# Loading an output projection as four consecutive rows per partition, in a kernel that streams a key and value cache

## The chip, the cores and the metric

The kernel runs on one core of one Trainium2 chip. The metric is the device time of one execution in microseconds (us). Before the change three runs gave a median of 1267.47 us (1267.24 to 1267.68). A profile records one execution: its "span" runs from the first to the last instruction and is some 2 us shorter than the time quoted for the same run (1266.8 against 1268.64 us before the change).

## The reference, cut to what matters

One token passes through attention over a cache of 65,536 positions, and beside it through a small gated network, which the change doesn't touch.

```python
Hq, Hkv, Sk, Dh = 16, 8, 65536, 256      # 16 query heads, 8 key/value heads
q = (x @ wq).reshape(B, Sq, Hq, Dh).transpose(0, 2, 1, 3)
scores = einsum("bhqd,bhkd->bhqk", q, repeat(k_cache, 2, axis=1)) * Dh ** -0.5
o = einsum("bhqk,bhkd->bhqd", softmax(scores), repeat(v_cache, 2, axis=1))
a = o.transpose(0, 2, 1, 3).reshape(B, Sq, Hq * Dh) @ wo      # wo is 4096 x 448, bf16
return g * a + (1 - g) * b
```

Keys and values are 537 MB in bf16 and each byte is read once. `wo` is 3.7 MB.

## The kernel before

The work goes through 8 pairs of query heads (`REP = 2` heads share one key/value head), four tiles each, 32 tiles in all. A tile is 8 MB of keys and 8 MB of values. SyncE issues all large loads, in this order:

```python
for j in range(NP):                       # 32 tiles
    if j >= 1:
        eng.wait_ge(sem_tr[NB - 1], BODY * (j - 1) + DC)   # half of the last tile's keys are read
    load(kring, A_k_cache, j, ...)        # 8 MB
    ...
    eng.wait_ge(sem_pv, j)                # the last tile's values are used up
    load(vbuf, A_v_cache, j, ...)         # 8 MB
    ...
    if j % PPH == 0:                      # first tile of a head pair
        g = j // PPH
        if g >= 1:
            eng.wait_ge(s_proj, g)        # the last head pair's projection is done
        eng.dma_start(wo_sb[:, :, :],
                      A_wo[g * REP * DH:(g + 1) * REP * DH, :].rearrange(
                          "(h p j) n -> p h (j n)", h=REP, j=2)).then_inc(sem_wo, 16)
```

So partition `p` of `wo_sb` gets rows 2p and 2p+1 of the first head of the pair and rows 2p and 2p+1 of the second. These are two stretches of 1792 B, read 229 KB apart and written side by side.

At the end of a head pair the sums over the positions lie in `accs`. Two fp32 products bring them into columns, one column per head and parity of d. VectorE divides them by the softmax sums, and 16 small products multiply them with `wo`:

```python
def by_d(dst):                                        # TensorE
    for dj in range(2):
        ins = pe.matmul(dst[:, dj * REP:(dj + 1) * REP], accs[:, dj:DH:2], sel[:, :], ...)
    return ins
def project():
    for hh in range(REP):
        for dj in range(2):
            j = dj * REP + hh
            for q in range(NCG):
                ins = pe.matmul(prj[32 * q:32 * q + 1, 0:WG], oTn[:, j:j + 1],
                                wo_sb[:, hh, dj * DM + q * WG:dj * DM + (q + 1) * WG], ...)
    ins.then_inc(s_proj, 1)

def finish_head(g):                                   # VectorE
    take(...)                                         # accs, densum, rden = 1 / densum
    vec.tensor_copy(qcur[:, :, :], qT[:, :, bass.ds(g * REP + REP, REP)])
    vec.drain()
    vec.wait_ge(s_sel, g + 1)
    by_head(acc[:, SELC:NACC])                        # oTn = sums * rden
```

Below, "head" means one such pair.

The softmax here doesn't subtract the row's maximum and nothing guards it: scores larger than these inputs give would overflow.

Of the kernel before, what the change touches and what calls it, by code (L numbers as in the profile page):

```python
# [8 lines left out]
ALU = mybir.AluOpType  # L9
# [3 lines left out]
def bass_gated_mix__gqa_block_cached__mixer_token_mlp__decode_kernel(  # L13
# [15 lines left out]
    f32 = mybir.dt.float32  # L29

    H = A_k_cache.shape[1]
    T = A_k_cache.shape[2]
    DH = A_k_cache.shape[3]
    DM = A_x.shape[-1]
    HQ = A_wq.shape[1] // DH
    REP = HQ // H
    F = B_w1.shape[1]
    FT = F // 128
    P = 128
# [28 lines left out]
    NCG = 4  # L68
    WG = DM // NCG
# [15 lines left out]
    SELC = DENC + 2 * NT  # L85
    NACC = SELC + 2 * REP
# [4 lines left out]
    with ctx:  # L91
        def sb(shape, dt, name):
            return ctx.enter_context(nc.sbuf_tensor(name, shape, dt))

        def psum(shape, dt, name):
            return ctx.enter_context(nc.psum_tensor(name, shape, dt))

        def new_sem(name):
            return ctx.enter_context(nc.semaphore(name))
# [11 lines left out]

        wo_sb = sb([P, REP, 2 * DM], bf16, "wo_sb")

        early = vbuf[:, :, :].rearrange("p n d -> p (n d)")
        early_f = vbuf_f[:, :, :].rearrange("p n d -> p (n d)")
        wq_a = early[:, 0:WF * NQ].rearrange("p (j n) -> p j n", j=WF)
# [23 lines left out]
        oTn = sb([P, 2 * REP], bf16, "oTn")  # L140
        accs = sb([P, SELC], f32, "accs")
        sel = sb([P, REP], f32, "sel")
        zrow = sb([1, NACC], bf16, "zrow")
        rden = sb([P, REP], f32, "rden")
        densum = sb([P, REP], f32, "densum")
        b2_b = sb([1, 1], bf16, "b2_b")
        stat = sb([1, 8], f32, "stat")
        statb = sb([1, 8], bf16, "statb")
# [16 lines left out]
        acc = psum([P, 512], f32, "acc")  # L165
        prj = psum([P, 512], f32, "prj")
# [8 lines left out]
        sem_wo = new_sem("sem_wo")  # L175
# [8 lines left out]
        s_sel = new_sem("s_sel")  # L184
# [14 lines left out]
        s_oTn = new_sem("s_oTn")  # L199
# [9 lines left out]
        def src(cache, j, n0=0, n1=NV):  # L209
            g, m = divmod(j, PPH)  # L210
            s = cache[0, g, m * BODY * CH:(m + 1) * BODY * CH, :].rearrange("(p n) d -> p n d", p=P)
            return s[:, n0:n1, :].rearrange("p n d -> p (n d)")

        @block.sync
        def _(eng):
            eng.dma_start(wq_a.rearrange("p j n -> p (j n)"),  # L216
                          A_wq[0:WF * P, :].rearrange("(p j) n -> p (j n)", p=P)).then_inc(sem_wq, 16)
            eng.dma_start(wq_b, A_wq[WF * P:DM, :].rearrange("r (a n) -> (r a) n", a=2)  # L218
                          ).then_inc(sem_wq, 16)
            def load(dst, cache, j, n0, n1, at, sem):  # L220
                eng.dma_start(dst[:, at + n0:at + n1, :].rearrange("p n d -> p (n d)"), src(cache, j, n0, n1)  # L221
                              ).then_inc(sem, 16)

            for j in range(NP):
                last = j == NP - 1
                if j >= 1:
                    eng.wait_ge(sem_tr[NB - 1], BODY * (j - 1) + DC)
                load(kring, A_k_cache, j, 0, HV if last else NV, HV * (j % 2), sem_k)
                if last:
                    load(kring, A_k_cache, j, HV, NV, HV, sem_kb)  # L230
                if j == 0:
                    eng.wait_ge(s_q, 1)
                    eng.wait_ge(s_hb, 1)
                else:
                    eng.wait_ge(sem_pv, j)
                load(vbuf, A_v_cache, j, 0, NLATE if last else NV, 0, sem_v)
                if last:
                    for (n0, n1), sem in zip(pieces, sem_vp):
                        load(vbuf, A_v_cache, j, n0, n1, 0, sem)
                if j % PPH == 0:  # L240
                    g = j // PPH
                    if g >= 1:
                        eng.wait_ge(s_proj, g)
                    eng.dma_start(wo_sb[:, :, :],
                                  A_wo[g * REP * DH:(g + 1) * REP * DH, :].rearrange(
                                      "(h p j) n -> p h (j n)", h=REP, j=2)).then_inc(sem_wo, 16)
            eng.wait_ge(s_fin, 1)
            eng.dma_start(out_ap, out_g[0:P:P // NCG, :]).then_inc(sem_out, 16)
            eng.wait_ge(sem_out, 16)
# [13 lines left out]
        def _(pe):  # L263
# [76 lines left out]
            def piece_wait(n):  # L340
                for (n0, _), sem in zip(pieces, sem_vp):
                    if n == n0:
                        pe.wait_ge(sem, 16)
# [11 lines left out]
            def by_d(dst):  # L355
                for dj in range(2):
                    ins = pe.matmul(dst[:, dj * REP:(dj + 1) * REP], accs[:, dj:DH:2], sel[:, :],
                                    start=False, stop=True, skip_group_check=True)
                return ins

            def clear(bank):
                pe.matmul(bank, ones_sq[0:1, :], zrow[0:1, 0:bank.shape[-1]], start=True, stop=True,
                          skip_group_check=True)

            def project():
                for hh in range(REP):
                    for dj in range(2):
                        j = dj * REP + hh
                        for q in range(NCG):
                            ins = pe.matmul(prj[32 * q:32 * q + 1, 0:WG], oTn[:, j:j + 1],  # L370
                                            wo_sb[:, hh, dj * DM + q * WG:dj * DM + (q + 1) * WG],
                                            start=False, stop=True, skip_group_check=True)
                ins.then_inc(s_proj, 1)


            def tail():
                late_values(*pieces[0])
                pe.wait_ge(s_cp, H)
                by_d(sps[:, 0, 0:2 * REP])
                late_values(pieces[1][0], NV).then_inc(s_late, 1)  # L380
                pe.wait_ge(sem_wo, 16 * H)
                pe.wait_ge(s_oTn, H)
                project()

            pe.sem_inc(sem_qk, 2)
            pe.wait_ge(sem_ident, 1)
# [11 lines left out]
            for dj in range(2):  # L398
                for h in range(HQ):
                    j = dj * HQ + h  # L400
                    col = h * DH
                    a, cb = divmod(col, HALF)
                    for kt in range(WF):
                        pe.matmul(sps[:, 1, j:j + 1], wq_a[:, kt, col + dj:col + DH:2],
                                  xcol[:, kt:kt + 1], start=(kt == 0), stop=False)
                    ins = pe.matmul(sps[:, 1, j:j + 1], wq_b[:, cb + dj:cb + DH:2],
                                    xcol[:, WF + a:WF + a + 1], start=False, stop=True)
# [13 lines left out]
            with nc.Fori(0, H, 1, engines=on, head_slot={pe.engine: 0}) as g:  # L421
                with nc.Fori(0, PPH, 1, engines=on, head_slot={pe.engine: 0}) as m:
                    j = pe.snap(g * PPH + m, min_val=0, max_val=NP - 1)
                    c0 = pe.snap(j * BODY, min_val=0, max_val=NC)
                    u16 = pe.snap(j * 16 + 16, min_val=16, max_val=16 * NP)
                    keys(c0, j, u16, pe.snap(x2_reg, min_val=0, max_val=NV))
                    values(j, c0, u16)
                    with pe.If(j < FT):
                        pe.wait_ge(s_pb, j + 1)
                        for q in range(NCG):  # L430
                            pe.matmul(prj[32 * q:32 * q + 1, WG:2 * WG], w2cur[:, :],  # L431
                                      gu[:, q * WG:(q + 1) * WG], start=False, stop=True, skip_group_check=True)
                    pe.reg_sub(x2_reg, NV, x2_reg)
                with pe.If(g < H - 1):
                    pe.wait_ge(s_cp, g + 1)
                    clear(acc[:, 0:NACC])
                    by_d(acc[:, SELC:NACC]).then_inc(s_sel, 1)
                    pe.wait_ge(sem_wo, pe.snap(g * 16 + 16, min_val=16, max_val=16 * H))
                    pe.wait_ge(s_oTn, g + 1)
                    project()  # L440

        @block.vector
        def _(vec):
# [101 lines left out]
            def by_head(src):  # L545
                po_v = src.rearrange("p (dj hh) -> p dj hh", dj=2, hh=REP)
                r_v = rden[:, :].rearrange("p (o hh) -> p o hh", o=1).broadcast_to((P, 2, REP))
                vec.tensor_tensor(oTn[:, :].rearrange("p (dj hh) -> p dj hh", hh=REP), po_v, r_v,  # L548
                                  op=ALU.mult).then_inc(s_oTn, 1)

            def finish_head(g):
                take(vec.snap(g * PPH + PPH, min_val=PPH, max_val=NP))
                vec.tensor_copy(qcur[:, :, :], qT[:, :, bass.ds(g * REP + REP, REP)])
                vec.drain()
                vec.wait_ge(s_sel, g + 1)
                by_head(acc[:, SELC:NACC])

            vec.wait_ge(s_q, 1)
            vec.tensor_copy(qT[:, :, :].rearrange("p a b -> p (a b)"), sps[:, 1, 0:2 * HQ])
# [8 lines left out]
            with nc.Fori(0, H - 1, 1, engines=on) as g:  # L568
                with nc.Fori(0, PPH, 1, engines=on) as m:
                    j = vec.snap(g * PPH + m, min_val=0, max_val=NP)  # L570
# [12 lines left out]
            with nc.Fori(NC - NCPH, NC, BODY, engines=on) as c0:  # L583
                for k in range(BODY):
# [6 lines left out]
                                     op0=ALU.mult, op1=ALU.add).then_inc(s_fin, 1)  # L591
# [69 lines left out]
```

## Time and profile before

| | |
|---|---|
| time, median of 3 | 1267.47 us |
| span of the profiled execution | 1266.8 us |
| duration of the packet records, summed, per DMA engine | 1261.7 us |
| TensorE busy | 911.8 us (72%) |
| one tile, from key landing to key landing | 38.70 us; 39.90 us where a wo load lies between |

The page of the kernel before, from its slice, queue and group parts. The DMA row gives tenths of busy time in 40 slices of the span. A group line gives, after the first bar, busy us and mean ns of one instruction, and after the second the idle time ahead of them and what ended most of it:

```profile
DMA  9999999999999999999999999999999999999998
DMA packets 12365, 544.39 MB, mean 430 GB/s; under 512 B 1344, under 2 KB 3394, under 8 KB 3778
q1 hardware_dynamic: 12264, 544.22, 99.5%
q8 instruction: 8, 0.13, 0.0%
L278 PE MATMUL kst<-ident,kring 128*128 128x128 f32 x4096 | 561.6, 298 | 310.5 <-DMA kring<-in_A_k_cache_dram 308.6
```

The DMA engines are busy throughout (9 tenths or more in every slice but the last; the packets of q1 took 99.5% of the span), and TensorE waits 308.6 us in total for key loads. The kernel is bound by its transfers.

The chain of waits of the kernel before, at three successive tiles. Columns: start in us, duration in us, what ran:

```profile
190.25 6.14 PE kst L278 x32
...
230.15 6.66 PE kst L278 x32
...
268.86 6.09 PE kst L278 x32
```

The keys of a tile are read as soon as they land (0.12 us later in this chain), so the differences are the time that the transfers of one tile take: 39.90 us with the wo load in between, then 38.71 us without. This step is the ruler of this study. It repeats within 0.02 us from head to head, while whole runs differ by 0.4 us and more.

The timeline of the kernel before, at the end of the first head (the number in brackets is idle time ahead of the instruction, and what ended it):

```profile
180.73 0.55 PEld L357 LDWEIGHTS acc<-sel,accs 128*128 128x128 f32 x4
181.78 0.37 PE L370 MATMUL prj<-wo_sb,oTn 128*1 128x112 bf16 x16 [0.41 <-DVE oTn L548]
182.19 0.38 SPq L244 DMA_DIRECT2D wo_sb<-in_A_wo_dram  x1
190.25 1.97 PE L278 MATMUL kst<-ident,kring 128*128 128x128 f32 x8 [8.10 <-DMA kring<-in_A_k_cache_dram]
```

After the projection TensorE has nothing to do for 8.1 us.

### The profile page before, as it was taken

How to read it: one execution, taken by the hardware profiler on the slowest of the kernel's cores; microseconds unless marked ns; L12 is line 12 of the kernel's file. 1: busy time of each engine (PE TensorE's matmuls, PEld its weight loads, DVE VectorE, ACT ScalarE, POOL GpSimd, SP SyncE). 2: the span in 40 equal slices, each digit the busy share in tenths (PEclk: the TensorE clock that was granted, in tenths of full speed). 3: DMA queues.
4: the chain of work that ended last, by engine and by line, in shares of the span. 5: the costliest groups of instructions: out<-in, count | busy, mean ns of one | idle time of the engine just before them, and what ended most of it. 6: DMA issues, size and time to landing. Idle time of an engine off the chain costs nothing.

```text
span 1266.8 us, 38663 instructions
## 1 busy us (share of the span) xinstructions
PE 911.8 (72%) x17041; PEld 862.0 (68%) x17041; DVE 418.1 (33%) x741; ACT 537.4 (42%) x786; POOL 0.9 (0%) x7
## 2 busy tenths in 40 slices
PE   1886678766787666787666876768767688666698
PEld 1776668766677666686666876658766578665687
DVE  2433334333344233443222332223322233331233
ACT  0543345533355333454334553335533345432455
POOL 0000000000000000000000000000000000000000
PEclk9988789788898788888788888789887788887989
DMA  9999999999999999999999999999999999999998
GB/s 411 430 417 430 432 430 441 430 432 432 430 441 430 432 430 432 441 430 432 430 432 441 430 432 430 432 441 430 430 432 430 443 430 430 432 430 443 430 416 350
DMA packets 12365, 544.39 MB, mean 430 GB/s; under 512 B 1344, under 2 KB 3394, under 8 KB 3778
## 3 DMA queue, kind: packets, MB, share of 16 engines
q1 hardware_dynamic: 12264, 544.22, 99.5%
q8 instruction: 8, 0.13, 0.0%
q10 hardware_dynamic: 90, 0.01, 0.0%
q14 instruction: 3, 0.02, 0.0%
HBM read 544.22 MB, written 0.00 MB: 430 GB/s over the span
## 4 chain that ended last, share of the span: by engine, by line
DMA 68%; PE 30%; issue 1%; SPq 0%; DVE 0%; ACT 0%; ACTq 0%
DMA kring<-in_A_k_cache_dram 66%; PE kst L278 25%; PE sps L298 5%; DMA vbuf<-in_A_v_cache_dram 2%; PE acc L330 1%; PE sps L350 0%; SPq L221 0%; PE acc L322 0%; PE prj L370 0%; ACT pT L615 0%; SPq L218 0%; SPq L216 0%; DVE out_g L590 0%; PE prj L431 0%; DVE oTn L548 0%
## 5 line engine op out<-in xcount | busy, mean ns | idle before, releaser
L278 PE MATMUL kst<-ident,kring 128*128 128x128 f32 x4096 | 561.6, 298 | 310.5 <-DMA kring<-in_A_k_cache_dram 308.6
L626 ACT ACTIVATE ktT<-kst 128x1024 bf16<-128x1024 bf16 x512 | 499.6, 1021 | 668.1 <-PE kst L278 667.8
L278 PEld LDWEIGHTS kst<-ident,kring 128*128 128x128 f32 x4096 | 511.8, 155 | 320.2 <-issue 318.0
L532 DVE COPY ktT<-kst 128x1024 bf16<-128x1024 bf16 x512 | 354.3, 692 | 771.4 <-PE kst L278 748.1
L298 PEld LDWEIGHTS sps<-qcur,ktT 128*128 128x128 bf16 x8192 | 237.8, 96 | 6.5 <-issue 3.9
L298 PE MATMUL sps<-qcur,ktT 128*128 128x2 bf16 x8192 | 236.7, 163 | 3.5 <-issue 3.5
L330 PE MATMUL acc<-vbuf,pT 128*2 128x256 bf16 x4064 | 144.2, 310 | 3.5 <-issue 2.8
L330 PEld LDWEIGHTS acc<-vbuf,pT 128*2 128x2 bf16 x4064 | 107.4, 95 | 31.9 <-issue 3.3
L615 ACT ACTIVATE pT<-sps 128x32 f32 x256 | 51.8, 202 | 18.6 <-PE sps L298 18.6
L322 PE MATMUL acc<-pT,ones_sq 128*128 128x32 bf16 x256 | 11.7, 178 | 12.3 <-ACT pT L615 12.3
L322 PEld LDWEIGHTS acc<-pT,ones_sq 128*128 128x128 bf16 x256 | 8.6, 97 | 15.2 <-ACT pT L615 14.9
L632 ACT ACTIVATE z_b<-z_b 128x448 bf16<-128x448 bf16 x14 | 8.1, 577 | 20.5 <-DVE z_b L519 20.5
L537 DVE COPY accs<-acc 128x288 f32<-128x288 f32 x8 | 3.7, 458 | 39.6 <-PE acc L330 39.6
L394 PE MATMUL acc<-vbuf 42*128 42x42 bf16 x1 | 0.2, 216 | 8.6 <-DMA b_b<-in_B_b_dram 8.6
L523 DVE TENSOR_SCALAR z_b<-z_b 128x448 bf16<-128x448 bf16 x14 | 3.9, 277 | 6.8 <-ACT z_b L632 6.8
L394 PEld LDWEIGHTS acc<-vbuf 42*128 42x128 bf16 x1 | 0.1, 100 | 8.7 <-DMA b_b<-in_B_b_dram 8.7
L525 DVE TENSOR_TENSOR gu<-wtmp,z_b 128x448 bf16<-128x448 bf16 x14 | 5.5, 393 | 1.0
L517 DVE TENSOR_TENSOR z_b<-u_b,wtmp 128x448 bf16<-128x448 bf16 x14 | 5.5, 393 | 1.0
L513 DVE TENSOR_TENSOR z_b<-wtmp,u_b 128x448 bf16<-128x448 bf16 x14 | 5.5, 393 | 1.0
L511 DVE TENSOR_TENSOR wtmp<-u_b 128x448 bf16<-128x448 bf16 x14 | 5.5, 392 | 1.1
L507 DVE TENSOR_SCALAR wtmp<-hbT,params 128x448 bf16<-128x448 bf16 x14 | 4.7, 337 | 2.6 <-issue 2.6
L509 DVE TENSOR_SCALAR u_b<-wtmp,params 128x448 bf16<-128x448 bf16 x14 | 4.7, 336 | 2.6 <-issue 2.6
(84 smaller groups left out, 76.5 us busy)
## 6 DMA issues: line engine op xcount, KB each, us to landing
kring<-in_A_k_cache_dram SPq DMA_DIRECT2D x2, 4096.0 KB, 22.7
vbuf<-in_A_v_cache_dram SPq DMA_DIRECT2D x1, 6144.0 KB, 24.3
wo_sb<-in_A_wo_dram SPq DMA_DIRECT2D x8, 448.0 KB, 28.6
vbuf<-in_A_wq_dram SPq DMA_DIRECT2D x1, 3072.0 KB, 10.3
vbuf<-in_A_v_cache_dram SPq DMA_DIRECT2D x1, 1024.0 KB, 26.4
vbuf<-in_A_v_cache_dram SPq DMA_DIRECT2D x1, 768.0 KB, 27.4
vbuf<-in_A_wq_dram SPq DMA_DIRECT2D x1, 512.0 KB, 11.1
kring<-in_A_k_cache_dram SPq DMA_DIRECT2D x31, 27.9
```

What stands on the lines that cost most here:

```text
L278: ins = pe.transpose(kst[:, b, i * P:(i + 1) * P], kring_f[:, at + NT * (k % DC) + 4 * b + i, :], ident[:, :])
L298: ins = pe.matmul(sps[:, par, 2 * nt:2 * nt + 2], ktT[:, par, b, ntl * DH + dj:(ntl + 1) * DH:2], qcur[:, dj, :], start=(dj == 0), stop=(d ...
L322: pe.matmul(acc[:, DENC:SELC], ones_sq[:, :], pT[:, r, :], start=False, stop=(r == BODY - 1), skip_group_check=True)
L330: ins = pe.matmul(acc[o:o + REP, 0:DH], pT[:, r, 2 * nt:2 * nt + 2], vbuf[:, n, :], start=False, stop=False, skip_group_check=True)
L511: vec.tensor_tensor(W, U, U, op=ALU.mult)
L513: vec.tensor_tensor(Z, W, U, op=ALU.mult)
L517: vec.tensor_tensor(Z, U, W, op=ALU.add)
L525: vec.tensor_tensor(gu[:, :], W, Z, op=ALU.mult).then_inc(s_pb, 1)
L532: vec.tensor_copy(ktT[:, k % KTB, b, :], kst_b[:, b, :]).then_inc(sem_ev[b], 1)
L615: act.activation(pT[:, bass.ds(p0 + k % DC, 1), :].rearrange("p o n -> p (o n)"), sps[:, k % 2, 0:2 * NT], AF.Exp, scale=scale).then_inc(s ...
L626: act.activation(ktT[:, k % KTB, b, :], kst_b[:, b, :], AF.Copy).then_inc(sem_ev[b], 1)
L632: act.activation(z_b[:, :], z_b[:, :], AF.Tanh).then_inc(s_tanh, 1)
```

## The change

It aims at fewer and larger packets: for heads 0 to 6 a partition gets four consecutive rows of `wo`, 3584 B, in one piece. Partitions 0 to 63 then belong to the pair's first head and 64 to 127 to its second, so the head sums are laid out to match, which takes 8 narrow products instead of 2. The last head keeps the old form.

```diff
+        wo_rows = wo_sb[:, :, :].rearrange("p h n -> p (h n)")
+        HP = P // REP
...
+        rrow = sb([P, 1], f32, "rrow")
...
-                    eng.dma_start(wo_sb[:, :, :],
-                                  A_wo[g * REP * DH:(g + 1) * REP * DH, :].rearrange(
-                                      "(h p j) n -> p h (j n)", h=REP, j=2)).then_inc(sem_wo, 16)
+                    w = A_wo[g * REP * DH:(g + 1) * REP * DH, :]
+                    if g < H - 1:
+                        eng.dma_start(wo_rows, w.rearrange("(p i) n -> p (i n)", i=2 * REP)).then_inc(sem_wo, 16)
+                    else:
+                        eng.dma_start(wo_sb[:, :, :], w.rearrange("(h p j) n -> p h (j n)", h=REP, j=2)
+                                      ).then_inc(sem_wo, 16)
...
+            def by_row(dst):
+                for hh in range(REP):
+                    for i in range(2 * REP):
+                        ins = pe.matmul(dst[hh * HP:(hh + 1) * HP, i:i + 1], accs[:, i:DH:2 * REP],
+                                        sel[:, hh:hh + 1], start=False, stop=True, skip_group_check=True)
+                return ins
...                                                    # project takes the order of columns; wo_rows in place of wo_sb
-                    by_d(acc[:, SELC:NACC]).then_inc(s_sel, 1)
+                    by_row(acc[:, SELC:NACC]).then_inc(s_sel, 1)
...
-                    project()
+                    project(range(2 * REP))
...
+                for hh in range(REP):
+                    h = slice(hh * HP, (hh + 1) * HP)
+                    vec.tensor_copy(rrow[h, :], rden[h, hh:hh + 1])
+                vec.drain()
                 vec.wait_ge(s_sel, g + 1)
-                by_head(acc[:, SELC:NACC])
+                vec.tensor_scalar(oTn[:, :], acc[:, SELC:NACC], rrow[:, :], None, op0=ALU.mult).then_inc(s_oTn, 1)
```

More of the change, by code (lines that the diff above doesn't have):

```diff
@@ L112, in bass_gated_mix__gqa_block_cached__mixer_token_mlp__decode_kernel @@
         wo_sb = sb([P, REP, 2 * DM], bf16, "wo_sb")
+        wo_rows = wo_sb[:, :, :].rearrange("p h n -> p (h n)")
+        HP = P // REP
+        assert 2 * REP * HP == DH
         early = vbuf[:, :, :].rearrange("p n d -> p (n d)")
@@ L363, in clear, with project @@
                           skip_group_check=True)
-            def project():
-                for hh in range(REP):
-                    for dj in range(2):
-                        j = dj * REP + hh
-                        for q in range(NCG):
-                            ins = pe.matmul(prj[32 * q:32 * q + 1, 0:WG], oTn[:, j:j + 1],
-                                            wo_sb[:, hh, dj * DM + q * WG:dj * DM + (q + 1) * WG],
-                                            start=False, stop=True, skip_group_check=True)
+            def project(cols):
+                for i, j in enumerate(cols):
+                    for q in range(NCG):
+                        ins = pe.matmul(prj[32 * q:32 * q + 1, 0:WG], oTn[:, j:j + 1],
+                                        wo_rows[:, i * DM + q * WG:i * DM + (q + 1) * WG],
+                                        start=False, stop=True, skip_group_check=True)
                 ins.then_inc(s_proj, 1)
@@ L382, in tail @@
                 pe.wait_ge(s_oTn, H)
-                project()
+                project([dj * REP + hh for hh in range(REP) for dj in range(2)])
             pe.sem_inc(sem_qk, 2)
@@ L436, in _ @@
                     clear(acc[:, 0:NACC])
-                    by_d(acc[:, SELC:NACC]).then_inc(s_sel, 1)
+                    by_row(acc[:, SELC:NACC]).then_inc(s_sel, 1)
                     pe.wait_ge(sem_wo, pe.snap(g * 16 + 16, min_val=16, max_val=16 * H))
                     pe.wait_ge(s_oTn, g + 1)
-                    project()
+                    project(range(2 * REP))
         @block.vector
```

## The prediction

> **What bounds the kernel now.** The transfers. In the slice view the mean busy share of the 16 DMA engines is 9 tenths or more in all slices but the last; the queue table gives one queue 99.5% of the span. The packet records' durations add up to 1261.7 us for each of 16 engines in a span of 1266.8 us. The chain of waits is 66% "DMA kring<-in_A_k_cache_dram". PE transposes sat idle 308.6 us for the key loads, 31 times: about 10 us in every 38.7 us tile. On the timeline at a head's end PE finishes the projection near 182 us and then idles 8.1 us until the next keys land. A key load lands 27.9 us after its issue but occupies the engines only about 19.4 us (8 packets of 65536 B per engine, 2.42 us each), so some 8.5 us of work is queued ahead of each.
>
> **What the change removes.** A wo load before: 256 packets of 1792 B, mean 76.7 ns, 16 per engine: 1.23 us. The chain agrees: successive tiles' transposes start 38.70 us apart, and 39.90 us where a wo load lies between. After: 128 packets of 3584 B, 8 per engine. The trace has 2048 B packets at 84.8 ns and 4096 B packets at 159.0 ns; interpolated (an estimate), 3584 B takes 140.5 ns. So two packets (153.3 ns) become one: 12.9 ns saved, 0.10 us per load, 0.72 us for seven. The same two sizes leave about 10.6 ns a packet that doesn't depend on its bytes. [...] at 1792 B it is only about 14%. The bytes stay the same, so there is little to win.
>
> **What it adds.** Seven times: the head-sum products go from 2 fp32 matmuls (4 passes, 0.63 us together) to 8 narrow ones, 16 passes, an estimate of 1.2 to 2.5 us; two small VectorE copies and a drain, about 0.4 us (0.17 us a copy there), which overlap these; one tensor_scalar for one tensor_tensor. Together 1 to 2 us per head's end, which falls into PE's idle 8.1 us. The wo load is issued that much later, but waits over 20 us in the queue anyway (issued at 182.2 us, its packets start at 207.2 us). Nothing of it reaches the critical path. The last head's tail keeps its instructions and order.
>
> **Prediction.** 1267.47 - 0.72 = 1266.75 us; 8 times in 10 between 1265.9 and 1267.6. The run-to-run spread of before (0.44 us) is over half the effect. Chances: faster by over 2% 0.005, within 2% 0.99, slower by over 2% 0.005.
>
> **What would show the steps.** Packets under 2 KB fall by 1792; 896 of 3584 B appear at 138 to 144 ns; a head's first step between tiles falls from 39.90 to about 39.80 us, the others stay 38.70; summed DMA busy time per engine falls by 0.7 us. The projection at a head's end starts 1 to 2 us later, PE's idle time before the next keys and the time from wo issue to landing shrink as much.
>
> **What would make it wrong.** Head-end work beyond the 8.1 us slack (for instance an instruction fetch on PE in the first pass, where "issue" gaps of 2.8 us occur); a 3584 B packet slower than interpolated; a difference between chips above 1 us.

The sum: 1267.47 - 0.72 = 1266.75 us. The "it" is the 10.6 ns, 14% of the 76.7 ns of a 1792 B packet.

## The result, and the profile after

Six runs of the changed kernel gave a median of 1267.35 us (1267.15 to 1268.38); six runs of the kernel before, 1267.49 us (1267.24 to 1269.57). The ratio is 0.9998 with a 95% interval of 0.9986 to 1.0011: the same. Ratios here and below are the mean time of one kernel's fast runs over that of the other's of the same rounds, so not quite the ratio of the quoted medians. All results are correct unless said otherwise.

The page of the changed kernel, the same parts:

```profile
DMA packets 11469, 544.39 MB, mean 430 GB/s; under 512 B 1344, under 2 KB 1602, under 8 KB 2882
q1 hardware_dynamic: 11368, 544.22, 99.6%
L288 PE MATMUL kst<-ident,kring 128*128 128x128 f32 x4096 | 559.8, 298 | 303.4 <-DMA kring<-in_A_k_cache_dram 302.1
L375 PE MATMUL acc<-sel,accs 128*64 128x1 f32 x112 | 11.4, 260 | 0.0
```

Packets under 2 KB fell by 1792 as meant. The chain of waits of the changed kernel at the same tiles:

```profile
188.85 5.94 PE kst L288 x32
...
228.69 6.48 PE kst L288 x32
...
267.39 5.92 PE kst L288 x32
```

The step with the wo load is now 39.84 us, the next one 38.70. Heads 1 to 6 show 39.82 to 39.84 us, against 39.90 to 39.91 before. So a load became cheaper by 0.08 us. The summed packet records fell from 1261.7 to 1260.9 us per engine, near the predicted 0.7 us.

The timeline of the changed kernel at the end of the first head:

```profile
179.11 1.54 PEld L375 LDWEIGHTS acc<-sel,accs 128*64 128x64 f32 x16
181.14 0.37 PE L386 MATMUL prj<-wo_sb,oTn 128*1 128x112 bf16 x16 [0.41 <-DVE oTn L576]
181.56 0.33 SPq L253 DMA_DIRECT2D wo_sb<-in_A_wo_dram  x1
188.85 5.39 PE L288 MATMUL kst<-ident,kring 128*128 128x128 f32 x27 [7.34 <-DMA kring<-in_A_k_cache_dram]
```

The sums' weight loads take 1.54 us instead of 0.55, and TensorE's idle time before the next keys shrank from 8.10 to 7.34 us. Nothing else moved there.

**Why 0.5 us is lost in the runs' spread.** Seven loads at 0.08 us make 0.56 us, yet the medians differ by 0.14. In the spans, measured from the third tile's key landing (112.73 us before, 111.33 us after) to the end, the kernel before takes 1266.8 - 112.73 = 1154.07 us and the changed one 1265.0 - 111.33 = 1153.67 us: 0.40 us less, near the 6 x 0.08 us that this stretch holds. The first two tiles differ by 1.4 us between these two executions, and by up to 2 us over the profiles of kernels with the same loads in them. In the kernel before, TensorE stood still several times in its first pass through the tile loop. Three lines from the timeline there:

```profile
58.37 1.84 PE L298 MATMUL sps<-qcur,ktT 128*128 128x2 bf16 x64 [2.62 <-issue]
65.77 4.34 PE L330 MATMUL acc<-vbuf,pT 128*2 128x256 bf16 x95 [2.77 <-issue]
72.98 0.26 PE L431 MATMUL prj<-gu,w2cur 128*1 128x112 bf16 x4 [2.87 <-issue]
```

Near these stops the packet records show single instruction packets of 16,384 B (at 55.7, 63.4 and 70.2 us, 1.02 to 1.08 us each); while one runs, 15 packets of the loads are mostly under way instead of 16, so it takes an engine from them. In this execution the values of the next tile were issued so late (at 70.15 us) that the queue ran short, with fewer than 12 packets under way at 70.6 to 71.4 us. In the profile of the changed kernel it did not. (The profiled execution of the kernel before took 1268.64 us, over a microsecond above that kernel's median.) This fits the spread of the runs, but no experiment was spent on it.

### The profile page after: what moved, and what is told of

Its sections match the earlier page's. It is cut to its first block, busy times and chain, and to the rows that moved or that the text cites. A ratio compares the mean times of both kernels' runs of the same rounds, so it can differ in the third digit from the quotient of the medians.

```text
span 1265.0 us, 38851 instructions
## 1 busy us (share of the span) xinstructions
PE 918.8 (73%) x17124; PEld 868.1 (69%) x17125; DVE 420.6 (33%) x755; ACT 536.9 (42%) x786; POOL 0.9 (0%) x7
## 4 chain that ended last, share of the span: by engine, by line
DMA 71%; PE 29%; issue 0%; SPq 0%; DVE 0%; ACT 0%; ACTq 0%
DMA kring<-in_A_k_cache_dram 68%; PE kst L288 24%; PE sps L308 4%; DMA vbuf<-in_A_v_cache_dram 2%; PE acc L340 0%; PE sps L360 0%; SPq L228 0%; PE prj L386 0%; SPq L225 0%; SPq L223 0%; PE acc L332 0%; DVE out_g L610 0%; ACT pT L635 0%; DVE oTn L564 0%; ACTq L635 0%
## 5 line engine op out<-in xcount | busy, mean ns | idle before, releaser
L375 PEld LDWEIGHTS acc<-sel,accs 128*64 128x64 f32 x112 | 10.8, 214 | 0.9
L375 PE MATMUL acc<-sel,accs 128*64 128x1 f32 x112 | 11.4, 260 | 0.0
```

Source lines behind the costliest of these rows:

```text
L375: ins = pe.matmul(dst[hh * HP:(hh + 1) * HP, i:i + 1], accs[:, i:DH:2 * REP], sel[:, hh:hh + 1], start=False, stop=True, skip_group_check= ...
```

## The experiments

Theories, as they stood after the first look. **A**: every packet has a fixed part that shows in the time, so halving the packets brings the 0.08 us. **B**: only bytes count. **C**: the longer head sums cost time and eat part of the gain. The first four runs led to **D** (two far sources read in turn are slow), and these to **F** (the start address in SBUF decides) and **G** (the gap between two packets in SBUF decides). The theories and letters are those of the expectations quoted below.

### 1. More loads of wo, in one piece or two

```diff
+                if j < NP - PPH:
+                    if j >= 1:
+                        eng.wait_ge(sem_more, 16 * 4 * j)
+                    w = A_wo[(j // PPH) * REP * DH:(j // PPH + 1) * REP * DH, :]
+                    for r in range(4):            # more_four; more_two: "(p a i) n -> p a (i n)", a=2, i=2,
+                        eng.dma_start(wo_more[:, r, :],          # into pieces 32 B apart
+                                      w.rearrange("(p i) n -> p (i n)", i=2 * REP)).then_inc(sem_more, 16)
```

> The changed kernel with 112 further loads of wo into a scratch tile (four in each of the first 28 key tiles), each as 128 packets of 3584 B. Theory A (each packet has a fixed part which nothing hides, since the engines are busy throughout): a load costs what its packets take in the trace of the changed kernel, 8 x 143.6 ns = 1.149 us, so 112 x 1.149 = +128.7 us, about 1396 us. Rival B (only bytes count, fixed parts of packets overlap): the bytes at the rate of the key loads, 458752 B at 433 GB/s = 1.06 us, so +118.7 us, about 1386 us, and the same as with two packets a partition.

> The same 112 further loads and the seven true ones, but each as 256 packets of 1792 B (a gap of 32 B between the two halves of a partition's rows in SBUF keeps the packets apart). Theory A: 119 x 1.229 - 7 x 1.149 = +138.2 us over the changed kernel, about 1405.5 us, 9.5 us more than with packets of 3584 B (119 x 0.080). Rival B: no difference between the two.

Measured: 1394.8 us with 3584 B packets (4 runs), 1400.23 us with 1792 B packets (4 runs). The difference is 5.4 us, so B is wrong: the form of the packets shows in the time. But A asked for 9.5 us. Over 119 loads it is 0.046 us each, a little over half of what the change brought per load.

### 2. Very small packets

The seven loads in pieces of 224 B, with a gap of 32 B after each in SBUF.

```diff
+        wo_cut = sb([P, 2 * REP * 4, DM // 4 + 16], bf16, "wo_cut")
...
-                        eng.dma_start(wo_rows, w.rearrange("(p i) n -> p (i n)", i=2 * REP)).then_inc(sem_wo, 16)
+                        eng.dma_start(wo_cut[:, :, 0:DM // 4], w.rearrange("(p i) (c n) -> p (i c) n", i=2 * REP, c=4)).then_inc(sem_wo, 16)
...                                                    # the products read wo_cut
```

> The changed kernel with the seven wo loads in 2048 packets of 224 B each (the same rows, head sums and products; a gap of 32 B after each 224 B in SBUF). Theory A with the line from 2048 B and 4096 B packets (10.6 ns fixed): 18.7 ns a packet, 128 per engine, 2.4 us a load, 7 x 1.25 = +8.7 us over the changed kernel, about 1276 us. [...] Rival B (only bytes count): no change.

Measured: 1277.28 us (4 runs; 1.0074 of the kernel before, interval 1.0058 to 1.0089), and 41.12 to 41.16 us for the first steps of heads 2 to 6 (40.68 for head 1), so about 2.44 us a load. B is wrong here too, and the straight line of the prediction gave the right size (2.4 us). But this run doesn't count packets alone. `wo_cut` begins at byte 201,696 of a partition and its pieces follow every 256 B, so all of them start at 224 over a multiple of 256, which experiment 5 finds to be a bad place (7.8 ns a packet of 1792 B there). The (2.44 - 1.14) / 120 = 10.8 ns for each of the 120 further packets of an engine hold both the price of a packet and that of a bad start.

### 3. Each half of the change alone

The new head sums, with wo in two packets a partition (32 B apart in SBUF):

```diff
+        wo_gap = sb([P, 2, 2 * DM + 16], bf16, "wo_gap")
...
-                        eng.dma_start(wo_rows, w.rearrange("(p i) n -> p (i n)", i=2 * REP)).then_inc(sem_wo, 16)
+                        eng.dma_start(wo_gap[:, :, 0:2 * DM], w.rearrange("(p a i) n -> p a (i n)", a=2, i=2)).then_inc(sem_wo, 16)
...                                                    # the products read wo_gap
```

> The changed kernel's head sums and rows, but wo in 256 packets of 1792 B again (a gap of 32 B between two halves of a partition's rows in SBUF). Theory A: 7 x 0.08 = +0.56 us over the changed kernel, equal to the kernel before within the noise of some 0.3 us; a head's first step between tiles back at 39.91 us, the others 38.70 us. Rival C (the longer head sums cost about 0.4 us of the time and hide most of the gain): 0.4 us above the kernel before, and the steps at a head's end above 39.91 us.

And the new load with the old head sums (the rows don't match the sums then, so its result was meant to be wrong; the comparison with the reference passed it all the same):

```diff
+                    if g < H - 1:
+                        eng.dma_start(wo_sb[:, :, :].rearrange("p h n -> p (h n)"),
+                                      w.rearrange("(p i) n -> p (i n)", i=2 * REP)).then_inc(sem_wo, 16)
```

> The kernel before with only the loads of the change (four consecutive rows a partition, 3584 B packets) and the old head sums; wrong result on purpose, since sums and rows no longer match. If the longer head sums of the change cost nothing: the first steps of heads 39.83 us, as in the changed kernel, others 38.70; about 0.07 us per head less than the kernel before. If the head sums cost something, these steps are below 39.83 us. A PE idle before the next keys at a head's end of about 8.3 us, against 7.3 us in the changed kernel.

Measured: 1268.19 us for the sums alone (5 runs), 1268.51 us for the loads alone (4 runs), both within 0.05% of the kernel before. The medians can't tell 0.5 us. The steps can. The chain of waits of the run with the sums only:

```profile
190.77 5.83 PE kst L289 x32
...
230.60 6.38 PE kst L289 x32
```

and of the run with the loads only:

```profile
188.96 6.05 PE kst L282 x32
...
228.79 6.61 PE kst L282 x32
```

Both steps are 39.83 us, that of the changed kernel. For the loads alone this was expected: the head sums cost nothing, and C is out. (From the third key landing to the end this run takes 1265.1 - 111.43 = 1153.67 us, the same as the changed kernel. TensorE's idle time before the next keys was 8.21 us; 8.3 had been expected.) For the sums alone it was a surprise. They use 256 packets of 1792 B, as the kernel before does, yet the whole gain is there. A in its simple form is wrong: **the gain does not need fewer packets.** Two things differ from the kernel before in that load: its sources are adjacent, and its second packet is written 32 B further on.

### 4. Adjacent or far sources

54 further loads, each alone between two 8 MB loads. `lone_four` uses 3584 B packets, `lone_two` 1792 B from adjacent addresses, `lone_far` 1792 B read 229 KB apart; the last two write to the same places.

```diff
+                if 1 <= j < NP - PPH:              # behind the key load; once more behind the value load, into wo_more[:, 1]
...
+                    eng.dma_start(wo_more[:, 0, :, 0:2 * DM], w.rearrange("(h p j) n -> p h (j n)", h=REP, j=2)).then_inc(sem_more, 16)
```

> The changed kernel with 54 further loads of wo, each alone between two 8 MB loads (one after the key load and one after the value load of tiles 1 to 27), as 128 packets of 3584 B. The steps of the changed kernel say 1.13 us for such a load: 54 x 1.13 = +61 us, about 1328.4 us.

> The same 54 loads as 256 packets of 1792 B, the two of a partition read from adjacent addresses and written 32 B apart. Theory A (every packet has a fixed part that shows in the time): 54 x 0.08 = 4.3 us more than with 3584 B. Theory D (what the change removed was reading two far places in turn, 229 KB apart; adjacent packets cost almost nothing more, as the 39.84 us step of the run with the sums only says): at most 0.01 to 0.02 us a load, 0.5 to 1 us more in all.

> The same 54 loads as 256 packets of 1792 B written to the same places, but read as the kernel before reads them: a partition's two packets 229 KB apart. Theory A: as with adjacent addresses. Theory D: 1.20 us a load as in the steps of the kernel before, 54 x 0.07 = 3.6 us more than with adjacent addresses and 3.8 us more than with 3584 B.

Measured (5 runs each): 1328.67 us with one packet, 1330.37 us with two from adjacent addresses, 1330.67 us with two from far ones. The ranges of the last two overlap (1330.24 to 1330.72 and 1330.23 to 1331.07), and their steps agree at 41.04 us. D asked for 3.6 us between them, so D is wrong. A asked for 4.3 us between one packet and two, and 1.7 was measured. The destination was left.

### 5. Seven forms of one load in one run

One further load in each of 21 tiles, into a scratch tile whose start was chosen per form. The allocator puts `wo_sb` at byte 198,112 of each partition, which is 32 over a multiple of 64 (and 224 over a multiple of 256). The scratch tile starts with the same remainder; the "good" places are 32 B further on, at a multiple of 512.

```diff
...
+                    s, at, step = ((far, 0, 896), (far, 16, 896), (near, 0, 912), (far, 0, 928),
+                                   (four, 0, 0), (four, 16, 0), (far, 0, 912))[n % 7]      # in elements of 2 B
+                    d = wo_any[:, at:at + 2 * step].rearrange("p (a n) -> p a n", a=2)[:, :, 0:896] if step else wo_any[:, at:at + 1792]
+                    eng.dma_start(d, s).then_inc(sem_more, 16)
```

> The kernel before with one further load of wo in each of the 21 tiles between the heads' first tiles (head 7 left out), issued right behind the value load as the true one is, into a scratch tile; seven forms in turn, three times each. The step to the next tile, less 38.70 us, is the cost of that form. Forms: 0 two packets of 1792 B, sources 229 KB apart, written side by side from an SBUF address that is 32 over a multiple of 64 (the kernel before); 1 the same from a multiple of 64; 2 adjacent sources, second packet 32 B further on (the run with the sums only: one packet of each two at a multiple of 64); 3 far sources, second packet 64 B further on (neither at a multiple of 64); 4 one packet of 3584 B at 32 over a multiple of 64 (the changed kernel); 5 the same at a multiple of 64; 6 as 2 with far sources. Theory F (the SBUF address modulo 64 decides): form 0 and 3 at 1.20, forms 2 and 6 at 1.14, form 1 at 1.10 or so, form 5 below form 4 (1.13). Theory G (the gap between the two packets decides): forms 2, 3 and 6 at 1.14, forms 0 and 1 at 1.20, 5 as 4. Theory D, all but fallen (far sources decide): 0, 1, 3, 6 at 1.20, 2 at 1.14. Theory A (a packet's fixed part decides): 0, 1, 2, 3 and 6 alike, 0.08 above 4 and 5.

The chain of waits of this run, ten key loads in a row (start plus duration is the landing):

```profile
404.91 28.09 DMA kring<-in_A_k_cache_dram
443.65 29.27 DMA kring<-in_A_k_cache_dram
484.05 28.65 DMA kring<-in_A_k_cache_dram
524.41 28.19 DMA kring<-in_A_k_cache_dram
563.19 29.26 DMA kring<-in_A_k_cache_dram
603.55 28.80 DMA kring<-in_A_k_cache_dram
643.97 28.21 DMA kring<-in_A_k_cache_dram
682.71 29.38 DMA kring<-in_A_k_cache_dram
723.11 28.75 DMA kring<-in_A_k_cache_dram
763.46 28.23 DMA kring<-in_A_k_cache_dram
```

The landings are 433.00, 472.92, 512.70, 552.60, 592.45, 632.35, 672.18, 712.09, 751.86 and 791.69. Their differences are, in turn, form 0, form 1, a true load, forms 2, 3, 4, a true load, forms 5 and 6. The run is a single execution, so its state is unknown; the two steps with a true load in these lines, 39.90 and 39.91 us, are those of the kernel before. All repeats (the first of form 0 fell into the start-up and is left out):

| form | packets | packets starting at a bad place | step, us | less 38.70 |
|---|---|---|---|---|
| 0, kernel before | 256 of 1792 B | all | 39.92, 39.91 | 1.21 |
| 3, 64 B gap, far | 256 of 1792 B | all | 39.91, 39.90, 39.92 | 1.21 |
| 2, 32 B gap, adjacent (the run with the sums only) | 256 of 1792 B | half | 39.84, 39.85, 39.83 | 1.14 |
| 6, 32 B gap, far | 256 of 1792 B | half | 39.83, 39.83, 39.84 | 1.13 |
| 1, moved by 32 B | 256 of 1792 B | none | 39.80, 39.78, 39.79 | 1.09 |
| 4, changed kernel | 128 of 3584 B | all | 39.85, 39.83, 39.83 | 1.14 |
| 5, moved by 32 B | 128 of 3584 B | none | 39.76, 39.77, 39.76 | 1.06 |

This settles where the gain comes from. The gap is not the cause (form 3 has one and gains nothing; form 1 has none and gains most), nor are the sources (2 and 6 agree): the place where a packet starts in SBUF decides, as F says, though not by a multiple of 64 (below). In the step, a bad start costs (39.915 - 39.79) / 16 packets per engine = 7.8 ns a packet, or (39.837 - 39.763) / 8 = 9 ns for the larger ones. A packet by itself costs (39.79 - 39.763) / 8 = 3 ns in this run. (A step holds the load and what it does to the packets behind it, of which more below. These differ between forms 1 and 5, so the 3 ns is not clean. Experiment 6, where nothing starts badly, gives 4.7 ns.)

The change is form 0 to form 4, 0.08 us: it takes away 8 packets per engine and with them 8 bad starts. The two prices don't simply add. Form 2, which has the 8 fewer bad starts and as many packets as before, already costs what form 4 does, so on this way the starts bring everything; where all starts are good, 8 fewer packets bring 0.03 to 0.04 us. So the starts account for half of the change's gain at least, and how the rest divides isn't determined. **In this run, moving the tile by 32 B with packets as they were brought 0.125 us a load, more than the change did.**

The good places tested here were multiples of 256, and in the next run of 128; the bad ones lay 32 or 224 over a multiple of 256. F was put to the test as "a multiple of 64", but a start at 64 over a multiple of 128 is not among the forms.

Experiment 4 holds that case by accident. Its first load of a tile, between the key and the value landing, starts its two packets at 224 and 0 over multiples of 256, as form 2 does; its second, between the value and the key landing, at 32 and 64. By the landings in the trace of `lone_two` the first stretch takes 20.49 us on average and the second 20.54 (those without a true load behind), where both take 19.35 without a load: 1.14 us for the first load, as form 2, and 1.19 for the second, nearly as the forms with bad starts only. `lone_far` shows 20.49 and 20.56. `lone_four`, with one packet from 224 or from 32, shows 20.49 in both, so 32 is no worse than 224. A start at 64 over a multiple of 256 thus counts as bad, and what these runs support is a multiple of 128, not of 64.

It also accounts for a difference that the figures above leave open. They put two packets with one bad start 16 x 3 + 8 x 8 = 112 ns above nothing and one packet with a bad start 8 x 3 + 8 x 9 = 96 ns, so only 0.016 us apart, while the runs of experiment 4 had 1.7 / 54 = 0.031 us between these forms. With all starts of the second load bad, the table gives 0 for the first load and 1.21 - 1.14 = 0.07 for the second, 0.035 on average. In experiment 1 (0.046 us) two of the four pairs lay at 32 and 64 or at 160 and 192; that explains a part, and the rest stays open.

A bad start also slows what follows. In this run the packets of 65,536 B behind a load of form 1 took 2418.6 to 2418.8 ns on average, behind form 5 2420.1 to 2420.3, behind a true load (bad starts) 2421.8 in every head after the first. The key and value tiles had not moved. The records of the load itself don't show all of it: with half of the starts bad (forms 2 and 6) its packets took 74.1 ns, as with none, and only those behind were slower than behind form 1, 2421.4 to 2421.5 ns. No run tells why form 5, without a bad start, leaves slower packets than form 1.

### 6. The changed kernel, aligned

```diff
+        pad_a = sb([P, 192], bf16, "pad_a")       # keys and values from 128 over a multiple of 512 to a multiple of 512
         kring = sb([P, NV + HV, DH], bf16, "kring")
...
+        pad_b = sb([P, 16], bf16, "pad_b")        # wo from 32 over a multiple of 64 to 128 over a multiple of 256
         wo_sb = sb([P, REP, 2 * DM], bf16, "wo_sb")
```

> The changed kernel with the wo tile moved 32 B on in SBUF, to a multiple of 64 (all eight loads), and the key and value tiles moved from 128 over a multiple of 512 to a multiple of 512. If theory F holds in the real loads too: the first steps of heads 1 to 6 at 39.76 us instead of 39.83, that of head 7 (two packets a partition) at 39.79 instead of 39.92; 7 x 0.07 + 0.12 = 0.6 us less than the changed kernel in all, near 1266.7 us, which the run-to-run spread of the times may hide. Since the keys and values start at multiples of 64 in every kernel, their steps should stay 38.70 us; a larger multiple that mattered would lower them.

Measured: 1264.62 us (5 runs, 1264.39 to 1265.83) beside 1267.65 us for the kernel before (9 runs, 1267.31 to 1268.85); ratio 0.9975, interval 0.9961 to 0.9988. It is about 3 us below the kernel before and 2.7 below the median of the changed kernel, whose runs were made in other rounds; the ranges don't meet. That is clear, though far below 2%. I had expected 0.6 us less than the changed kernel. From its DMA view and chain of waits:

```profile
DMA packets 11469, 544.39 MB, mean 431 GB/s; under 512 B 1344, under 2 KB 1602, under 8 KB 2882
162.87 26.81 DMA kring<-in_A_k_cache_dram
200.97 28.41 DMA kring<-in_A_k_cache_dram
241.29 26.74 DMA kring<-in_A_k_cache_dram
```

The landings are 189.68, 229.38 and 268.03, so the step with wo is 39.70 us (39.70 to 39.78 over heads 1 to 6) and, as I had not expected, the step without one is 38.65 (38.60 to 38.67 over the run) instead of 38.70. In the packet records nearly every packet behind the start-up takes the same time: 74 ns for 1792 B, 140 for 3584 B, 2418 for 65,536 B (to the fifth and the ninety-fifth percentile). In the changed kernel these were 74 to 86, 140 to 151 and 2418 to 2429. Summed per engine the records fell from 1261.7 us before to 1258.7 us, and 2.0 us of those 3.0 belong to the 65,536 B packets, which make up most of the kernel. From the third key landing to the end the span is 1263.6 - 112.46 = 1151.14 us, 2.9 us less than before and 2.5 us less than in the changed kernel.

Head 7, which still loads two packets a partition, was expected at 39.79 us, and its step was 39.82. Since nothing starts badly in this run, it shows what a packet costs by itself. The landing of the last engine scatters here (39.70 to 39.78), but the records also hold 16 packets of 4 B that close every key load, and the mean of their times is steadier: its steps are 39.735 us for each of heads 1 to 6, 39.773 for head 7 and 38.638 without wo. So the load costs 1.135 us with two packets and 1.097 with one, (1.135 - 1.097) / 8 = 4.7 ns for each packet saved. The records alone say 2 x 74 - 140 = 8 ns; but 16 x 74 = 1184 ns of records fit into those 1135 ns, so neighbouring records overlap by some 3 ns, and a difference of durations overstates a packet's price.

What stays open: this run moved three tiles at once. The run with seven forms shows that good wo starts quicken the large packets behind them while keys and values stay put. Whether moving the keys and values added to it was not separated. In the run with seven forms the keys right behind a load of form 1 took 2418.0 ns, as here, but the values behind these 2419.3 to 2419.7, with no bad wo start in between, so their old places may have had a share.

### 7. How much work a head's end could hide

The prediction called TensorE's idle time at a head's end the limit. The first try added idle matmuls:

```diff
                     project(range(2 * REP))
+                    with nc.Fori(0, 5, 1, engines=on, head_slot={pe.engine: 0}):
+                        spin(10)
```

> The changed kernel with 50 idle matmuls of 128x512 (about 0.24 us each, 12 us in all) on TensorE after the projection at the end of heads 0 to 6. As the prediction put it, head-end work beyond the idle time before the next keys (7.3 us in the changed kernel) would show: 7 x 4.7 = +33 us. If the queue of loads behind is slack as well (each key load is issued some 8.5 us before its turn), 12 us is still inside 7.3 + 8.5 = 15.8 us: no change in the time, TensorE starts the next keys 4.7 us late, and the next key load's time from issue to landing falls from 28 to about 23 us.

Measured: 1361.22 us (4 runs), +94 us, more than any theory said. The queue part of its page and its timeline at the first head's end tell that the experiment measured something else:

```profile
q8 instruction: 72, 1.18, 0.3%
183.88 10.74 PE L324 MATMUL kst<-ktT,ones_sq 128*128 128x512 bf16 x45 [0.38 <-issue]
205.54 5.60 PE L288 MATMUL kst<-ident,kring 128*128 128x128 f32 x32 [10.91 <-issue]
```

72 instruction packets instead of 8 (1.18 MB instead of 0.13, so the 64 further ones are of about 16 KB too), and behind the added loop TensorE stood still another 10.91 us, waiting for no data. From the projection to the next keys it was 22 us, not 12, and the run says nothing about 12 us. That TensorE's instructions were fetched again and that it stood still for that reason is the author's reading of these two figures; why this loop should bring it, no run shows.

The second try put the delay on VectorE, ahead of the normalised sums:

```diff
+                for _ in range(28):
+                    vec.tensor_tensor(wtmp[:, :], u_b[:, :], u_b[:, :], op=ALU.mult)
+                    vec.drain()
+                vec.drain()
                 vec.wait_ge(s_sel, g + 1)
```

> The changed kernel with 28 products of 128x448 on VectorE (about 0.45 us each, 12 to 13 us in all) before the normalised head sums at the end of heads 0 to 6, in place of the spoiled run with idle matmuls; TensorE waits for them, so its projection comes 12 us later, without a loop on TensorE. As the prediction put it (slack is the idle 7.3 us before the next keys): 7 x 4 to 5 = +28 to +35 us. If the queue of loads is slack as well (8.5 us more): no change in the time beyond its spread, steps as in the changed kernel, the first keys of heads 1 to 7 read some 5 us after they landed.

Measured: 1273.68 us (4 runs, 1272.69 to 1275.82), about 6 us above the changed kernel and not 28 to 35. The timeline of this run at the first head's end:

```profile
181.83 12.99 DVE L576 TENSOR_TENSOR wtmp<-u_b 128x448 bf16<-128x448 bf16 x28
195.39 0.54 PE L386 MATMUL prj<-wo_sb,oTn 128*1 128x112 bf16 x16 [12.99 <-DVE oTn L580]
196.59 6.16 PE L288 MATMUL kst<-ident,kring 128*128 128x128 f32 x32 [0.66 <-issue]
207.94 0.33 SPq L228 DMA_DIRECT2D kring<-in_A_k_cache_dram  x1
```

VectorE hands over its sums 195.02 - 180.03 = 15.0 us after the value load was issued, against 180.78 - 178.37 = 2.4 us in the changed kernel: 12.6 us later. TensorE had 7.3 us to spare and began the next keys too late by the rest, yet the key load behind them, issued at 207.94 us, reached the engines when the queue had just begun to run dry: in the packet records fewer than 12 packets are under way from about 207.7 to 209.1 us, fewer than 5 for some 0.4 us of that. So the loads waiting in the queue hide delay as well, but not all of the 8.5 us I had given them. Here 12.6 us was just over the limit, at 0.9 us per head on average. In the key landings it is uneven: from the last one ahead of a head's end to the second one after it, the first two heads take 78.52 us, as without the delay (39.83 + 38.70), the other five 79.01 to 80.14.

## Why the prediction was right or wrong

- **The time and the verdict were right.** 1266.75 us was predicted and 1267.35 measured, inside the range of 1265.9 to 1267.6. The verdict "the same" came as expected. Neither says much: the time of the kernel before, 1267.47, lies inside the range too, so a gain of nothing would have fitted. What the prediction had right is in the steps.
- **The bound was right.** The kernel waits for its transfers, and the 0.08 us a load showed one to one in the step between tiles.
- **"Nothing of it reaches the critical path" was right, and tested.** With the new load and the old head sums the step is the same 39.83 us. The added work came to about 1 us a head, at the low end of the predicted 1 to 2.
- **The size was a little off.** "12.9 ns saved, 0.10 us per load, 0.72 us for seven" was 0.08 us a load. The interpolated 140.5 ns for a 3584 B packet is what such a packet takes when nothing disturbs it (140 in the aligned kernel); in the changed kernel it took 143.4 ns, since each still starts at a bad place.
- **The cause given was a part at most.** "The same two sizes leave about 10.6 ns a packet that doesn't depend on its bytes" took the whole difference for a price of packets. The runs say 3 to 4.7 ns for a packet and some 8 ns for a bad start, as they show in the step. Half of the change's 0.08 us at least came because half as many packets have half as many bad starts, and the run with the sums only has the whole gain with no fewer packets. The prediction also took "there is little to win" from it; the alignment that the change left untouched (of wo, keys and values together) was worth another 2.5 us.
- **"Head-end work beyond the 8.1 us slack" was not the limit.** The slack is the idle time plus a part of the queue; a delay of 12.6 us cost 0.9 us a head on average.
- **The spread was named but undersized.** 0.44 us came from three runs; six runs of the kernel before spread over 2.3 us, and much of that fits the first two tiles.

## What to carry to other kernels

Where the DMA engines never rest, as here (99.5% of the span), look at where each destination tile starts in SBUF before reshaping its packets: compare the packet durations, those of the loads behind it too, with the fastest of their size, and if they scatter upwards (in the changed kernel 74 to 86 ns for 1792 B and 2418 to 2429 for 65,536 B), try the tile at a multiple of 128 B. Here 32 B brought 0.125 of 1.21 us a load (form 0 against form 1), and the aligned kernel runs as many instructions as the changed one (38,851). A change far below the spread of the runs can still be judged from a repeated step inside one trace, such as the time from landing to landing. Test an attribution by undoing half of the change, because here the half that should have lost the gain kept it. And look up where a test's own scratch tiles start: in experiments 1 to 4 that place was a second variable.
